# Four zero fills of the cache gradients issued earlier: one behind the softmax, three in the steps of the N passes

## The chip, the cores and the metric

The kernel runs on one core of a Trainium2 chip. TensorE (PE) multiplies matrices, VectorE (DVE) and ScalarE (ACT) work element by element, GpSimd (POOL) and SyncE (SP) are used here almost only to issue DMAs. The DMAs of POOL form one queue (q0 in the profile), those of SP another (q1); both are served by the same 16 DMA engines, which copy between the chip's memory (HBM) and the on-chip buffer (SBUF), or inside HBM. The metric is device time in microseconds, lower is better. Three runs of the kernel before took 599.88, 599.93 and 602.61 us, the median is 599.93 us.

## The reference: what is computed

One token passes through a transformer block with adaptive layer norm, and the gradients of all its inputs are wanted. Cut to what matters:

```python
mod = (silu(c) @ w_mod).reshape(1, 6, 1, -1)      # sa, ca, ga, sb, cb, gb
h = layernorm(x) * (1 + ca) + sa
# attention: 32 query heads, 4 key/value heads, the last W = 4096 of 65536 cached rows
q = (h @ wq).reshape(1, 1, 32, 128)
k = repeat(k_cache[:, :, 65536 - W:, :], 8); v = repeat(v_cache[:, :, 65536 - W:, :], 8)
x = x + ga * ((softmax(q @ k.T * 128 ** -0.5) @ v) @ wo)
h = layernorm(x) * (1 + cb) + sb
x = x + gb * ((sigmoid(h @ w_gate) * (h @ w_up)) @ w_down)      # 1024 -> 3584 -> 1024
# outputs: x and the gradients of x, k_cache, v_cache, wq, wo, w_gate, w_up, w_down, c, w_mod
```

Only the last 4096 rows of the caches take part. So in the gradients of `k_cache` and `v_cache` (out_2 and out_3, 4 x 65536 x 128 in bf16 each) the first 61440 rows of each group are zero, and the kernel must write these zeros: 8 x 15.7 MB, about 126 MB of all the 185.6 MB that it writes to HBM.

## The kernel before

**Stages.** The program is written out by hand in one order for each engine (a manual schedule). Its stages in the profile are: loads, layer norm and the query projection (0 to about 50 us); scores and softmax (50 to 73 us); four N passes of 32 steps each, one pass for each key/value group (73 to 164 us); the B chunks, 64 pieces of 8 matmuls each, with the second layer norm and the modulation between them (164 to 314 us); the feed-forward turns `q` = 0 to 6, one for each 512 of the 3584 columns (320 to about 480 us); the outer products and stores that end the program (480 to 598 us).

**Zero fills.** The zeros are cut into 120 pieces of 1 MB in a list `zleft`. `zero(n, after, big)` (L180 to L208) takes the next `n` pieces and issues a DMA on POOL's queue for each. There are three forms. The plain one (L206) writes 1 MB from `zeros`, an SBUF tile of fp8 zeros that the DMA widens to fp32. With `big=True`, in the N steps and the B chunks, a piece of the `flat` kind is copied from an already zeroed stretch of HBM, with the same widening, so that 0.25 MB is read for 1 MB written (L200). Six pieces, at the positions `NARROW = (15, 45, 75, 93, 103, 113)` of the list, take two DMAs (L191 with 2.5 KB and L194 with 960 KB); the last piece, 119, takes five (L173, L178). A piece keeps its place in the list whatever the place in the program from which it is issued. Pieces 1 to 9 are not of the `flat` kind.

**Where fills are issued.** Tables say how many pieces go where: `Z_Q` in the query projection, `Z_SM` behind the softmax sum, `Z_N[s]` in step `s` = 0 to 127 of the N passes, `Z_B` in the B chunks, `Z_GA`, `Z_CB` and `Z_FOLD` between these and the feed-forward part, `Z_FFN[q]` at four places of turn `q`, `Z_END` behind. `spread(total, n)` deals `total` pieces evenly over `n` steps. Some fills wait for an engine, by an added dependency: the one behind the softmax for DVE's reciprocal `rsum` (L586), those of an N step for a matmul six N matmuls back (`recent(mm, 6)`), those of a B chunk for the chunk's matmul three back. All fills, and nearly all loads and stores, stand in POOL's one queue in program order: a DMA that waits holds up all that are behind it. POOL's DMAs use eight semaphores in turn, so a ninth is issued only when the one eight before it has landed.

**Loads behind the fills.** In POOL's queue, among the N fills and the B fills, stand `load_wo` (L375: `wo` 0, then 4 + g at the end of pass g, and 3), `b_sec` (L378: the sections of `w_mod`, 1 MB each) and the first `load_ug` (L960: `w_up` and `w_gate` of turns 0 and 1). Chunk 9 of the B chunks is the first that needs `wo` 3; `mod_rows(ga)` (L433) needs both `b_sec(2, ...)` loads; `mod_tiles` (L384) needs the first `b_sec(3, ...)` load.

**A feed-forward turn.** In turn `q`, for j = 0 to 7, DVE reduces a tile of `w_up` and `w_gate` (L250) and ACT or DVE overwrites it with its gradient (L281, L246). `store_ug(q, 0, 4)` (L964) follows j = 3, `store_ug(q, 4, 4)` follows j = 7; the fills `z[0]` and `z[1]` stand right behind them. At j = 4 `front(q + 1)` on PE (L1055) needs the `w_up` and `w_gate` of the next turn, which were loaded a turn before. Then come `hh_ops`, `ffn_mm` (L1073), `wd_ttr` and `wd_outer` for turn q + 1, which work on the two halves of `w_down`. There is one buffer for these: SP stores a half (L949), waits until it has landed, and only then loads the same half for the next turn (L946). At the end of turn `q`, `load_ug(q + 2)` waits for `store_ug(q)` to land, because it takes the same buffer:

```python
            if q + 2 < NB:
                load_ug(q + 2, 0, 4)
            wd_outer(q + 1, 1)
            zero(z[2])
            side()
            if q + 2 < NB:
                load_ug(q + 2, 4, 4)
            zero(z[3])
            if q + 2 < NB:
                load_wd(q + 2, 0)
                load_wd(q + 2, 1)
```

Of the kernel before, what the change touches and what calls it, by code (L numbers as in the profile page):

```python
# [41 lines left out]
def spread(total, n):  # L42
    return [(i + 1) * total // n - i * total // n for i in range(n)]
# [6 lines left out]
Z_CB = 1  # L50
Z_Q = [0] * 6 + [1, 3]
Z_KC = [0] * 8
Z_SM = 4
Z_N = spread(31, 128)
Z_B = [n + (i in (31, 38)) for i, n in enumerate(spread(29, 43))] + [1, 1, 1, 1, 0] + [1, 0, 0, 1, 1, 1, 0, 0] + [1, 0, 1, 0, 1, 0, 0, 0]
Z_FOLD = (1, 1, 1, 2)
Z_FFN = [(0, 2, 0, 2), (0, 2, 0, 1), (0, 2, 0, 2)] + [(0, 2, 0, 2)] * 2 + [(1, 1, 1, 3), (1, 2, 1, 0)]
Z_END = (1, 0, 0, 0, 0)
@with_exitstack
def kernel(  # L60
# [121 lines left out]
    def zero(n, after=None, big=False):  # L182
        for _ in range(n):
            if len(zleft) <= keep[0]:
                return
            region, narrow_ = zleft.pop(0)
            first = None
            if narrow_:
                nc.gpsimd.inc_swdge_sem([], [], mode="reset_dge_cursor")
                n = nlen - ncount.pop()  # L190
                first = nc.gpsimd.dma_start(  # L191
                    out=rest[0:NS, 0:nlen * 128].rearrange("p (t x) -> p t x", t=2)[:, :, n * 64:(n + 1) * 64],
                    in_=zeros[0:NS, 0:64].rearrange("p (t x) -> p t x", t=1).broadcast_to([NS, 2, 64]))
                ins = nc.gpsimd.dma_start(  # L194
                    out=region[8:P, :].bitcast(FP32).rearrange("(t p) x -> p t x", t=2),
                    in_=zeros[0:60, :].rearrange("p (t x) -> p t x", t=1).broadcast_to([60, 2, ZW // 2]))
            elif 119 - len(zleft) in UNEVEN:
                first = ins = uneven(region)
            elif big and region.shape[0] == 1:
                ins = nc.gpsimd.dma_start(  # L200
                    out=as_rows(region, BIGP).bitcast(FP32),
                    in_=zero_src[:, 0:P * ZW // 4].rearrange("i (p x) -> (i p) x", p=BIGP).bitcast(FP8))
            else:
                if region.shape[0] == 1:
                    region = as_rows(region, P)
                ins = nc.gpsimd.dma_start(out=region.bitcast(FP32), in_=zeros[:, :])  # L206
            if after is not None:
                dep(first or ins, after)  # L208
# [9 lines left out]
    def new_ps(name="ps"):  # L218
        p, tag = next_pool()
        return p.tile([P, 512], FP32, name=name, tag=tag)  # L220
# [365 lines left out]
    last = nc.vector.reciprocal(out=rsum, in_=ssum)  # L586
    zero(Z_SM, last)
    rs_ps = new_ps("rs_ps")[:, 0:P]
# [125 lines left out]
    def recent(mm, lag):  # L714
        last_mm.append(mm)
        return last_mm[-lag] if len(last_mm) >= lag else last_mm[0]

    for g in range(G):
        nbank = bank_pair("n_ps", g)
        for t_ in range(KT):  # L720
# [7 lines left out]
            for k in range(2):  # L728
                mm = nc.tensor.matmul(nbank[k][:, :], lhsT=k_nat[:, g, t_ * DH:(t_ + 1) * DH],  # L729
                                      rhs=vp[:, t_ % 2, 4 * k:4 * k + 4, :].rearrange("p h d -> p (h d)"),  # L730
                                      start=(t_ == 0), stop=False)
            zero(Z_N[s], recent(mm, 6), True)
            if t_ == 20:
# [387 lines left out]
    for q in range(NB):  # L1121
        z = Z_FFN[q]
        more = q + 1 < NB
# [328 lines left out]
```

## Time and profile before

| What | Value |
|---|---|
| median of three runs | 599.93 us |
| the profiled execution, its own time | 600.48 us |
| its span in the profile | 598.7 us |
| PE, DVE, ACT, POOL busy | 68%, 61%, 43%, 26% of the span |
| moved by DMA | 246.55 MB, mean 412 GB/s |
| POOL's queue, SP's queue (packet time of 16 engines) | 91.4%, 12.8% |
| fills of the plain form (L206) | 45, each 1 MB, median 12.7 us from issue to landing |
| fills of the form in HBM (L200) | 68, median 10.5 us |
| `load_wo` (L375), sections of `w_mod` (L378) | median 8.1 us, 12.0 us |
| stores of `w_down` gradients (L949), loads of `w_down` (L946) | median 10.5 us, 9.6 us |

The packet time of a queue is the time that its packets took, from start to end, as a share of 16 engines' time. Packets of two queues on one engine overlap in it, so the two shares together can pass 100%. "To landing" is counted from the issue to the last of the 16 engines' completion marks, with the time in the queue in it.

### The profile page before, as it was taken

How to read it: one execution, taken by the hardware profiler on the slowest of the kernel's cores; microseconds unless marked ns; L12 is line 12 of the kernel's file. 1: busy time of each engine (PE TensorE's matmuls, PEld its weight loads, DVE VectorE, ACT ScalarE, POOL GpSimd, SP SyncE). 2: the span in 40 equal slices, each digit the busy share in tenths (PEclk: the TensorE clock that was granted, in tenths of full speed). 3: DMA queues.
4: the chain of work that ended last, by engine and by line, in shares of the span. 5: the costliest groups of instructions: out<-in, count | busy, mean ns of one | idle time of the engine just before them, and what ended most of it. 6: DMA issues, size and time to landing. Idle time of an engine off the chain costs nothing. (4 is left out here: it accounts for less than half of the span.)

```text
span 598.7 us, 9909 instructions
## 1 busy us (share of the span) xinstructions
PE 405.1 (68%) x4007; PEld 236.0 (39%) x4036; DVE 362.5 (61%) x677; ACT 259.3 (43%) x398; POOL 153.7 (26%) x258
## 2 busy tenths in 40 slices
PE   3997779998999999997975526254263254984020
PEld 2784433333334545544444525244253234631000
DVE  3765679988730111049266986677866878978160
ACT  3489512554540104311132755464655655893020
POOL 3113113211214113221321333324343154232000
PEclk9997789999999999997996556556555568855555
DMA  8999999999999999999999999999999999999997
GB/s 348 422 420 419 423 458 374 451 440 435 422 413 379 464 427 388 451 422 427 371 412 372 357 411 415 405 409 417 414 415 412 418 418 412 423 424 425 424 416 321
DMA packets 36461, 246.55 MB, mean 412 GB/s; under 512 B 6097, under 2 KB 6097, under 8 KB 21664
## 3 DMA queue, kind: packets, MB, share of 16 engines
q0 software_dynamic: 29120, 218.65, 91.4%
q1 hardware_dynamic: 7248, 27.27, 12.8%
q8 instruction: 31, 0.51, 0.3%
q14 instruction: 14, 0.11, 0.1%
q10 hardware_dynamic: 48, 0.01, 0.0%
HBM read 78.28 MB, written 185.60 MB: 441 GB/s over the span
## 5 line engine op out<-in xcount | busy, mean ns | idle before, releaser
L788 PE MATMUL b_ps<-arena 128*128 128x512 bf16 x493 | 116.1, 383 | 2.6 <-ACT arena L932 1.1
L932 ACT COPY arena<-tp_side 128x1024 bf16<-128x1024 bf16 x62 | 60.9, 1014 | 66.7 <-PE tp_side L931 66.7
L233 DVE TENSOR_TENSOR arena<-arena 128x2048 bf16<-128x2048 bf16 x64 | 77.7, 1224 | 9.0 <-PE n_ps L729 4.0
L250 DVE CUSTOM_DVE_ANT_0 arena<-arena,scr 128x1024 bf16<-128x1024 bf16 x56 | 66.2, 1220 | 9.3 <-ACT scr L1094 9.3
L788 PEld LDWEIGHTS <-arena 128*128 128x128 bf16 x512 | 48.9, 99 | 57.8 <-issue 5.0
L729 PE MATMUL n_ps<-arena 128*128 128x512 bf16 x246 | 66.3, 389 | 4.0 <-DVE arena L233 3.3
L931 PE MATMUL tp_side<-ident_bf,arena 128*128 128x128 bf16 x496 | 55.2, 290 | 13.2 <-DVE arena L233 5.6
L200 POOL DMA_DIRECT2D out_dram<-out_dram x68 | 33.7, 496 | 116.9 <-PE b_ps L788 56.6
L931 PEld LDWEIGHTS <-arena 128*128 128x128 bf16 x496 | 47.1, 135 | 19.2 <-issue 10.3
L1055 PE MATMUL fg<-h_bf,arena 128*128 128x1 bf16 x448 | 15.4, 166 | 48.4 <-DMA arena<-in_B_w_up_dram 29.1
L685 ACT CAST arena<-t_ps 128x512 bf16<-128x512 f32 x56 | 28.9, 598 | 39.9 <-PE t_ps L677 39.9
L281 ACT ACTIVATE arena<-scr,h 128x1024 bf16<-128x1024 bf16 x35 | 38.5, 1143 | 2.7 <-DVE dh2acc L250 2.3
L964 POOL DMA_DIRECT2D out_dram<-arena x28 | 22.1, 795 | 64.7 <-ACT arena L281 45.3
L206 POOL DMA_DIRECT2D out_dram<-zeros x45 | 25.1, 560 | 51.3 <-PE q_ps L433 14.2
L250 DVE CUSTOM_DVE_ANT_0 arena<-arena,b1k 128x1024 bf16<-128x1024 bf16 x24 | 28.4, 1221 | 15.9 <-PE fg L1073 15.9
L1272 ACT ACTIVATE arena<-ps_kv 128x512 bf16<-128x512 f32 x48 | 25.0, 714 | 29.3 <-PE ps_kv L1268 28.5
L1268 PE MATMUL ps_kv<-arena 32*128 32x512 bf16 x64 | 23.9, 546 | 20.1 <-DVE arena L246 19.2
L729 PEld LDWEIGHTS <-arena 128*128 128x128 bf16 x256 | 21.4, 99 | 35.8 <-issue 19.5
L242 DVE CAST arena<-b_ps 128x512 bf16<-128x512 f32 x6 | 4.2, 692 | 50.0 <-PE b_ps L788 50.0
L1055 PEld LDWEIGHTS <-arena 128*128 128x128 bf16 x448 | 13.8, 105 | 51.0 <-DMA arena<-in_B_w_up_dram 30.8
L677 PE MATMUL t_ps<-arena 128*32 128x512 bf16 x256 | 24.1, 399 | 3.4 <-ACT arena L752 2.8
L516 ACT COPY arena<-tp_wq 128x1024 bf16<-128x1024 bf16 x23 | 21.4, 1066 | 7.3 <-PE tp_wq L514 7.3
(314 smaller groups left out, 611.2 us busy)
## 6 DMA issues: line engine op xcount, KB each, us to landing
out_dram<-zeros POOLq DMA_DIRECT2D x45, 1024.0 KB, 12.7
out_dram<-arena POOLq DMA_DIRECT2D x28, 1024.0 KB, 18.6
out_dram<-arena POOLq DMA_DIRECT2D x30, 512.0 KB, 11.2
out_dram<-arena SPq DMA_DIRECT2D x20, 512.0 KB, 10.2
arena<-in_A_wq_dram POOLq DMA_DIRECT2D x8, 1024.0 KB, 21.2
arena<-in_A_wo_dram POOLq DMA_DIRECT2D x8, 1024.0 KB, 8.1
arena<-in_w_mod_dram POOLq DMA_DIRECT2D x7, 1024.0 KB, 12.2
arena<-in_B_w_up_dram POOLq DMA_DIRECT2D x14, 512.0 KB, 11.4
```

The lines of the kernel that those rows point to most:

```text
L200: ins = nc.gpsimd.dma_start(out=as_rows(region, BIGP).bitcast(FP32), in_=zero_src[:, 0:P * ZW // 4].rearrange("i (p x) -> (i p) x", p=BIGP ...
L206: ins = nc.gpsimd.dma_start(out=region.bitcast(FP32), in_=zeros[:, :])
L233: return nc.vector.tensor_tensor(out=out, in0=a, in1=b, op=op)
L250: return nc.vector.tensor_tensor_reduce(out=out, in0=w, in1=b, scale=1.0, scalar=0.0, op0=ALU.mult, op1=ALU.add, accum_out=acc)
L281: return nc.scalar.activation(out=out, in_=b, func=ACT.Copy, scale=col)
L685: nc.scalar.copy(out=o, in_=v)
L729: mm = nc.tensor.matmul(nbank[k][:, :], lhsT=k_nat[:, g, t_ * DH:(t_ + 1) * DH], rhs=vp[:, t_ % 2, 4 * k:4 * k + 4, :].rearrange("p h d -> ...
L788: mm = nc.tensor.matmul(bbank[p][k][:, :], lhsT=a4[:, p, h, :], rhs=wo_t[u][:, a, k * 512:(k + 1) * 512], start=(i == 0 and a == 0), stop= ...
L931: nc.tensor.transpose(tp[:, i * P:(i + 1) * P], blk[:, i * P:(i + 1) * P], ident_bf[:, :])
L932: nc.scalar.copy(out=blk if dst is None else dst, in_=tp[:, :])
L1055: nc.tensor.matmul(gu[:, col:col + 1], lhsT=ug_v[:, q % 2, j // 4, j % 4, k, f0:f0 + 255:2], rhs=h2_bf[:, j:j + 1], start=(j == 0 and i == ...
L1272: nc.scalar.activation(out=o, in_=v, func=ACT.Copy, scale=float(scale))
```

## The change

Four numbers in three tables. `Z_SM` goes from 4 to 5: one more fill behind the softmax. `Z_N` deals 34 fills over the 128 N steps, where it dealt 31. `Z_FFN` loses four: turns 0, 2, 3 and 4 issue one fill as `z[3]`, behind `load_ug(q + 2, 4, 4)`, where they issued two; turn 1 already had one. The counts of all other places stay.

```diff
-Z_SM = 4
-Z_N = spread(31, 128)
+Z_SM = 5
+Z_N = spread(34, 128)
 Z_B = [n + (i in (31, 38)) for i, n in enumerate(spread(29, 43))] + [1, 1, 1, 1, 0] + [1, 0, 0, 1, 1, 1, 0, 0] + [1, 0, 1, 0, 1, 0, 0, 0]
 Z_FOLD = (1, 1, 1, 2)
-Z_FFN = [(0, 2, 0, 2), (0, 2, 0, 1), (0, 2, 0, 2)] + [(0, 2, 0, 2)] * 2 + [(1, 1, 1, 3), (1, 2, 1, 0)]
+Z_FFN = [(0, 2, 0, 1)] * 5 + [(1, 1, 1, 3), (1, 2, 1, 0)]
```

Since the pieces keep their order, every place behind the softmax now issues pieces that stand further on in the list: by one at first, by four from the B chunks to turn 0, by none again from turn 5 on. So the N steps issue pieces 9 to 42 (before 8 to 38), and the narrow piece 93 leaves turn 0 and goes to the end of `Z_FOLD`. By form that makes 41 fills from SBUF (before 45) and 72 in HBM (before 68), with the same six narrow ones and the same last one.

## The prediction

> **What bounds the kernel now.** I read the slices of the page first, then busy time by stage, then the DMA issues of POOL and SP in order of time.
>
> ```profile
> DMA  8999999999999999999999999999999999999997
> ...
> 5.00:66.00 61.00, 49.02 (x677) 37.31 (x677) 34.83 (x71) 41.75 (x60) 13.60 (x25) 0.90 1.04 420
> 66.00:165.00 99.00, 90.10 (x575) 33.45 (x585) 83.03 (x89) 40.04 (x105) 21.15 (x42) 0.98 1.05 428
> 165.00:320.00 155.00, 141.60 (x1071) 72.47 (x1089) 50.55 (x104) 34.86 (x49) 37.85 (x66) 0.98 1.03 416
> 320.00:345.00 25.00, 13.83 (x261) 12.61 (x258) 22.77 (x49) 15.26 (x19) 8.18 (x12) 0.50 1.02 359
> 345.00:500.00 155.00, 69.61 (x1034) 59.07 (x1035) 114.75 (x259) 86.63 (x96) 54.11 (x77) 0.55 1.12 414
> 500.00:590.00 90.00, 40.93 (x397) 21.05 (x396) 55.93 (x106) 39.49 (x74) 17.63 (x29) 0.58 1.03 420
> ```
>
> Columns of the stages: bounds, length, busy time of PE, PEld, DVE, ACT, POOL, granted PE clock, DMA share, GB/s. The DMA engines are busy in every slice, at 414 to 428 GB/s in all stages but one; no compute engine is full for long. So the kernel ends when the DMA engines have moved its 246.55 MB, plus the time in which they had nothing to do. The stage with a hole is 320 to 345, the start of the feed-forward turns:
>
> ```profile
> 320.00:322.00 2.00, 1.62 (x61) 1.53 (x58) 1.95 (x5) 1.23 (x3) 0.00 (x0) 0.50 1.12 418
> 322.00:324.00 2.00, 0.99 (x32) 0.94 (x32) 1.62 (x6) 0.00 (x0) 0.13 (x1) 0.50 0.65 229
> 324.00:326.00 2.00, 0.00 (x0) 0.00 (x0) 1.95 (x4) 0.00 (x0) 0.42 (x1) 0.50 0.83 324
> 326.00:328.00 2.00, 1.76 (x16) 1.73 (x17) 1.03 (x4) 0.65 (x1) 0.66 (x2) 0.50 1.12 422
> 338.00:340.00 2.00, 0.53 (x20) 0.53 (x20) 1.69 (x7) 0.81 (x1) 0.17 (x1) 0.50 0.87 338
> 340.00:342.00 2.00, 2.00 (x34) 2.00 (x32) 2.00 (x3) 0.62 (x1) 2.00 (x4) 0.50 0.48 170
> 342.00:344.00 2.00, 1.21 (x10) 0.78 (x8) 2.00 (x5) 1.81 (x3) 2.00 (x3) 0.50 0.92 309
> ```
>
> The queues ran dry twice: POOL had issued everything and waited for DVE (8.59 us before its issue at 323.87) and ACT (6.53 us before 334.93). At 420 GB/s the five poor windows lost 2 x (191 + 96 + 82 + 250 + 111)/420 = 3.5 us (the 25 us stage as a whole: 25 x 61/420 = 3.6). Elsewhere short windows dip (262 and 206 GB/s in 184 to 188), but their neighbours make it up: 433, 287, 423, 549 GB/s in the four 5 us windows from 180 are 423 on average, since a packet is booked as a whole. I count 0 there, at most 0.7 (85 to 105 averages 405: 20 x 15/420).
>
> **The change, part by part.** (1) Four issues go from turns 0, 2, 3, 4 to 66-165 us. On POOL each costs 0.55 us from SBUF or 0.49 in HBM (L206, L200), and POOL is 21.15 of 99 us busy there: no cost. No bytes are written more or less. A fill in HBM reads 0.25 MB of HBM in place of SBUF; four of the form are added. At what speed? The N stage, mostly that form, moves 428 GB/s, the end, mostly stores from SBUF, 420: -0.05 to +0.2 us for each, taken as 0.
>
> (2) The N stage has no room for them: it issues 4 + 31 fills and 6 `load_wo`, 41 MB of 1.049, which at 428 GB/s is 100.5 us in 99 us. So the added 4.19 MB only lengthen the queue: all that stands behind on POOL's queue lands 4.19/0.42 = 10.0 us later (9.3 if 0.7 us of dips is filled), up to where the queue used to run dry. [...]
>
> (3) Who waits for the late loads? `wo` 3: issued 164.92, landed 8.4 us later at 173.3, then at 183.3; chunk 9 starts at 175.91 + 5 x 1.75 = 184.7 (seven chunks in 12.26 us): no stall. Second half of `ga`: 199.05 + 12.2 + 9.5 = 220.8, its matmuls wanted from 220.1: 0.7 us of PE. First half of `sb`: 252.76 + 10.0 + 9.5 = 272.3, wanted at 270.17: 2.1 us, but PE then stands 2.92 us for DVE at 275.78, which hides it. The last of `load_ug(1)`: 313.97 + 8.4 + 9.5 = 331.9, wanted by 331.6, in a chain that is itself late: 0. The compute chain reaches 322 us some 1 us late (0 to 4), while the queue is 9.3 to 10 us longer: DMA never stands still, so this costs the end nothing. Behind a full POOL queue the ninth DMA waits for its semaphore; what it holds up is in the same queue and would land no sooner.
>
> (4) The hole of 3.5 us is filled, since more than 5 us of queue remain: -3.5.
>
> (5) Turns 1 to 6 start late. With POOL's queue empty the first `store_wd` took 323.60 to 327.52 until its buffer could be loaded again, 3.9 us; under a full queue the next took 343.09 to 353.12, 10.0. The load then landed at 336.7 (9.2 us), and the next store left at 343.09; from a landed load to the store DVE needs 3.2 us (363.29 to 366.50, two L250 and two L246) and PE 0.5 before it, so 2.7 us of the delay are absorbed. The next turn comes about 1 + 6.1 - 2.7 = 4.4 us late. Meanwhile DMA, 3.5 us ahead in the end, needs the turns to follow. A turn's `w_down` loop is store 10.0, load 9.6, then 3.7 = 23.3 us; the five from 343.09 to 467.29 took 124.2. At 23.3 each they take 116.5: 4.4 - 7.7 = -3.3, as good as DMA's lead. With one fill less a turn moves 6.3 + 3.1 MB at 414 GB/s = 22.8 us, so loop and DMA are level. But turns of 23.4, 22.9 and 24.2 us were at the loop already and give nearly nothing back: at worst turn 5 is still 4.4 us late with DMA 3.5 ahead, 7.9 us. The queue that covers it: a `store_ug` landed 11.4 us after issue (median of 340 to 480, L964), 3.4 at the quickest, so 8.0 us of other work stood ahead of it. I take 0.3 us (0 to 3) of new holes.
>
> (6) The last of 16 engines decides. At the end the engines stop between 593.5 and 597 us (share 0.49 in 594 to 596, 0.05 behind); an engine that lags has lost less in the holes. Lost to this: 0.3 us (0 to 2).
>
> Sum on the profiled execution: 600.48 + 0 - 3.5 + 0.3 + 0.3 = 597.6. It lies 0.55 above the median of the runs, so 599.93 - 2.9 = **597.0 us**.
>
> ```profile
> 323.60 3.82 SPq L949 DMA_DIRECT2D out_dram<-arena  x2
> 327.52 3.09 SPq L946 DMA_DIRECT2D arena<-in_B_w_down_dram  x2
> 343.09 3.83 SPq L949 DMA_DIRECT2D out_dram<-arena  x2
> 353.12 2.92 SPq L946 DMA_DIRECT2D arena<-in_B_w_down_dram  x2
> 366.50 4.55 SPq L949 DMA_DIRECT2D out_dram<-arena  x2
> 377.24 4.52 SPq L946 DMA_DIRECT2D arena<-in_B_w_down_dram  x2
> 394.48 3.69 SPq L949 DMA_DIRECT2D out_dram<-arena  x2
> ```
>
> Columns: start, length, SP's queue and line, DMA. Each load of `w_down` follows its store by 10 us or so once the queue is full: that is the loop of step 5.
>
> **Rivals.** *The turns don't catch up (slower).* In the turn 366.50 to 394.48, 28.0 us, the loop was not the bound: the load had landed by 386.8 (377.24 + 9.6), and over all turns PE waited 29.1 us for `w_up` and 19.0 for `w_gate` (L1055). If turns 1 to 5 keep an average t, the change is 4.4 + 5t - 124.2, zero at t = 24.0; above that the engines stand idle for the fills that were moved away. At t = 24.6, between the loop's 23.3 and the 24.8 of before, nearer to the latter since a turn bound by other loads gains little, it is +3.2: 603.1 us. For it: two of five turns took 25.7 and 28.0. Against: that wait is time in the queue, and 1.05 MB less ahead of a load shortens it by 2.5 us. [...]
>
> *The hole only moves (no change).* Bytes are the same; if the thinner queue of turns 2 to 5 runs dry as often as turn 0 did, or the engine that ends last never idled in the hole, the 3.5 us come back: 599.9, within 1.2. For it: loop and DMA are level at 23 us. Against: the 8.0 us of reserve.
>
> *More is gained.* The 0.7 us of dips before 165 us go too, and nothing is lost in (5) and (6): 599.93 - 4.2 = 595.7. It needs every reserve to hold.
>
> **Chances.** Forecast 597.0 (own range 596.0 to 598.7): 0.50. Turns don't catch up, 602.0 to 605: 0.22. Hole moves, 598.7 to 601: 0.20. More gained, 595.3 to 596: 0.08. The bound of 0.5%, about what a measurement of this kernel can tell from no change, is 3.0 us: 596.93 and 602.93. Faster: 0.28 of the forecast, whose middle lies on the bound, and 0.08 = 0.36. Same: 0.22 of the forecast, all 0.20 of the second = 0.42. Slower: 0.22. The range runs from 595.5 to 603.4: it leaves out the upper part of the slower case and the last of the gain, some 0.15.
>
> **What would show it.** Right: no window of 2 us under 400 GB/s between 322 and 346; loads of `wo` and `w_mod` (L375, L378) land 6 to 10 us later after issue than 8.1 and 12.0; the first `store_wd` waits 10 us, not 3.9; the five turns from the second `store_wd` take 115 to 118 us; the mean rate rises to 414 GB/s. Wrong: windows well under 400 GB/s between 400 and 470 (the hole moved, or the turns don't catch up: then the five turns take over 120 us), or PE idle at L788 or L433 for many us before 320.

## The result and the profile after

| | before | after |
|---|---|---|
| median, runs beside each other | 600.06 us (599.88 to 602.61, 4 runs) | 593.69 us (593.46 to 594.23, 4 runs) |
| the profiled execution, its span | 600.48, 598.7 us | 593.46, 591.7 us |

The ratio is 0.9885, 95% interval 0.9858 to 0.9913: the change is faster, by 6.4 us in the medians and 7.0 us between the two profiled executions. The forecast was 597.0 us, range 595.5 to 603.4. Its direction was right; the gain was more than twice the 2.9 us forecast, and the time lies below the range.

The page of the profile after, its span, the DMA row of its slices, its DMA totals and two of its rows of DMA issues (count, KB of each, median us from issue to landing):

```profile
span 591.7 us, 9934 instructions
...
DMA  8999999999999999999999999999999999999998
...
DMA packets 36013, 246.55 MB, mean 417 GB/s; under 512 B 6097, under 2 KB 6097, under 8 KB 21664
...
arena<-in_A_wo_dram POOLq DMA_DIRECT2D x8, 1024.0 KB, 13.5
arena<-in_w_mod_dram POOLq DMA_DIRECT2D x7, 1024.0 KB, 19.0
```

The bytes are the same and the mean rate rose from 412 to 417 GB/s, more than the forecast's 414. In the median the loads behind the fills take 5.4 us (`wo`) and some 7 us (`w_mod`) longer from issue to landing than before; the forecast had named 6 to 10 us for both. The stages of the profile after (bounds, length, busy time of PE, PEld, DVE, ACT, POOL, granted PE clock, DMA share, GB/s):

```profile
5.00:66.00 61.00, 48.86 (x677) 37.23 (x677) 34.80 (x71) 41.66 (x59) 13.59 (x25) 0.90 1.04 420
66.00:165.00 99.00, 91.13 (x586) 33.39 (x585) 82.98 (x89) 40.08 (x105) 22.95 (x46) 0.98 1.05 431
165.00:320.00 155.00, 140.83 (x1074) 70.92 (x1072) 49.02 (x102) 34.90 (x48) 37.89 (x66) 0.99 1.03 423
320.00:345.00 25.00, 11.26 (x217) 10.28 (x215) 18.90 (x41) 12.34 (x16) 6.50 (x10) 0.50 1.14 403
345.00:500.00 155.00, 75.28 (x1138) 64.58 (x1138) 121.34 (x272) 93.09 (x105) 55.09 (x78) 0.56 1.10 412
```

The stage with the hole went from 359 to 403 GB/s. But the two stages ahead of it also went up, from 428 to 431 and from 416 to 423, and at 420 GB/s that is (99 x 3 + 155 x 7)/420 = 3.3 us (2.5 by the exact times below) for which the forecast had counted nothing. The five windows of 2 us that made the hole, in the profile after:

```profile
322.00:324.00 2.00, 1.56 (x59) 1.47 (x56) 1.53 (x6) 1.16 (x3) 0.00 (x0) 0.50 1.06 397
324.00:326.00 2.00, 0.99 (x32) 0.94 (x32) 1.62 (x6) 0.00 (x0) 0.19 (x1) 0.50 1.10 410
...
338.00:340.00 2.00, 1.01 (x8) 0.74 (x7) 1.96 (x4) 1.81 (x3) 0.41 (x1) 0.50 1.24 416
340.00:342.00 2.00, 0.00 (x0) 0.00 (x0) 1.48 (x6) 0.74 (x1) 0.24 (x1) 0.50 1.05 397
342.00:344.00 2.00, 0.00 (x0) 0.00 (x0) 0.00 (x0) 0.00 (x0) 2.00 (x4) 0.50 1.02 375
```

Before they moved 229, 324, 338, 170 and 309 GB/s. Three of the five are still a little under the 400 GB/s that the forecast had named as its sign, but the DMA share is above 1.00 in each. PE does nothing from 340 to 344 us, later than before, and the DMA engines work on all the same. The loop of `w_down` after (start, length, SP's queue and line):

```profile
325.54 3.81 SPq L949 DMA_DIRECT2D out_dram<-arena  x2
335.95 5.46 SPq L946 DMA_DIRECT2D arena<-in_B_w_down_dram  x2
348.72 4.31 SPq L949 DMA_DIRECT2D out_dram<-arena  x2
...
465.19 3.69 SPq L949 DMA_DIRECT2D out_dram<-arena  x2
```

The first store now waits 335.95 - 325.54 = 10.4 us, the next turn starts 5.6 us later than before (348.72 against 343.09), and the five turns take 116.5 us against 124.2, so that the last store leaves 2.1 us earlier.

**Where the time came from.** Two figures were worked out from the packet records of each trace. The *lead* of a kernel is the time at which the packets of the profile before had moved so many MB, less the time at which this kernel's had. *Lost time* is the time in which a DMA engine had no packet, as a mean over the 16 engines; where two packets overlap on one engine (the DMA share is 1.03 to 1.14 in the stages above) it hides the other's rest, so it is a lower bound.

| MB moved (time in the profile before) | 30 (74) | 40 (98) | 90 (216) | 130 (311) | 145 (351) | 190 (461) | 245 (592) | span |
|---|---|---|---|---|---|---|---|---|
| lead of after, us | 0.0 | 0.55 | 1.71 | 2.51 | 5.91 | 5.93 | 5.66 | 7.0 |

So 2.5 us were gained ahead of 311 us and 3.4 in the hole; 0.25 were lost again, all behind 461 us; and 1.4 were gained behind 592 us, where the engines run out. The lost time shows less than that:

| lost time, us | 85 to 100 us | 100 to 311 us | the hole, 311 to 351 us | behind 570 us |
|---|---|---|---|---|
| before | 0.20 | 0.50 | 2.64 | 2.3 |
| after | 0.00 | 0.00 | 0.02 | 1.0 |

### The profile page after: what moved, and what is told of

It reads as the page before. It is cut to its first block, busy times and chain, and to the rows that moved or that the text cites. A ratio compares the mean times of both kernels' runs of the same rounds, so it can differ in the third digit from the quotient of the medians.

```text
span 591.7 us, 9934 instructions
## 1 busy us (share of the span) xinstructions
PE 406.7 (69%) x4036; PEld 236.4 (40%) x4036; DVE 361.8 (61%) x677; ACT 259.9 (44%) x398; POOL 153.3 (26%) x258
## 4 chain that ended last, share of the span: by engine, by line
DMA 37%; PE 32%; DVE 14%; ACT 8%; issue 4%; POOL 0%; ACTq 0%; DVEq 0%; POOLq 0%; SPq 0%
DMA out_dram<-out_dram 10%; DMA out_dram<-arena 9%; PE n_ps L729 9%; DMA arena<-in_B_w_gate_dram 7%; DMA arena<-in_w_mod_dram 6%; PE b_ps L788 4%; DVE arena L250 4%; DVE arena L246 4%; PE t_ps L677 4%; DMA out_dram<-zeros 3%; ACT arena L516 2%; DVE arena L233 2%; PE tp_side L931 2%; PE bc_ps L337 1%; DMA arena<-in_B_w_down_dram 1%
## 5 line engine op out<-in xcount | busy, mean ns | idle before, releaser
L729 PE MATMUL n_ps<-arena 128*128 128x512 bf16 x256 | 67.7, 388 | 3.6 <-DVE arena L233 3.3
L200 POOL DMA_DIRECT2D out_dram<-out_dram x72 | 35.5, 494 | 128.2 <-PE n_ps L729 54.3
L206 POOL DMA_DIRECT2D out_dram<-zeros x41 | 23.0, 565 | 43.1 <-PE q_ps L433 14.3
```

The lines of the kernel that those rows point to most:

```text
L200: ins = nc.gpsimd.dma_start(out=as_rows(region, BIGP).bitcast(FP32), in_=zero_src[:, 0:P * ZW // 4].rearrange("i (p x) -> (i p) x", p=BIGP ...
```

## The experiments

Each kernel was timed beside the kernel before on the same chip, in a few series; a difference with a sign is worked out from the ratio. The median of before is 600.06 us beside the change and 601.69 to 602.11 us in the later series, so kernels of two series are best compared by their traces. Lines of the diffs are against the changed kernel; `...` marks what is left out, and what isn't shown is as there. Three theories were tested. *Queue*: the end follows from the time that the engines lose wherever POOL's queue is short, and any place ahead of these serves for the fills. *Hole*: only the stretch of 320 to 345 us counts. *Lighter turns*: the turns gain because they hold less.

**Two fills in place of four**, into the N steps, from turns 3 and 4.

```diff
-Z_SM = 5
-Z_N = spread(34, 128)
-Z_FFN = [(0, 2, 0, 1)] * 5 + [(1, 1, 1, 3), (1, 2, 1, 0)]
+Z_SM = 4
+Z_N = spread(33, 128)
+Z_FFN = [(0, 2, 0, 2), (0, 2, 0, 1), (0, 2, 0, 2)] + [(0, 2, 0, 1)] * 2 + [(1, 1, 1, 3), (1, 2, 1, 0)]
```

> Two fills move, from turns 3 and 4 into the N passes (33 instead of 31). Theory Q (queue): what counts is DMA time lost anywhere before 350 us while POOL's queue is short, 5.9 us in all in the kernel before, and each moved fill buys back 2.5 us of it until it is used up. Then two fills give -5.0 us (-4 to -5.5). Theory H (hole only): only the hole at 320 to 345 us counts, 3.5 us, and the rest of the -6.4 us comes from something else in the change; two fills fill the hole, so -3.5 us (-3 to -4). Theory T (lighter turns): the gain comes from each of turns 0, 2, 3, 4 having one fill less, 1.6 us each; two turns give -3.2 us.

596.55 us, ratio 0.9924 (0.9906 to 0.9942), -4.6. A little more than the hole alone should give, as the queue theory had it. Its lead is only 3.8 us at 351 us, and 0.66 us are still lost in the hole.

**Four fills put close ahead of the hole**, into the last B chunks; softmax and N steps as before the change.

```diff
-Z_SM = 5
-Z_N = spread(34, 128)
+Z_SM = 4
+Z_N = spread(31, 128)
-Z_B = ... + [1, 0, 0, 1, 1, 1, 0, 0] + ...
+Z_B = ... + [1, 1, 1, 1, 1, 1, 1, 1] + ...
```

> The same four fills leave the same turns, but go to B chunks 49, 50, 54 and 55 (about 280 to 300 us) instead of the softmax and the N passes. Theory Q: the hole at 320 to 345 is filled and what is lost from 285 on, but the 1.7 us that the engines had lost by 285 us stay lost: -4.3 us (-3.5 to -5). Theory H: -3.5 us plus the unknown rest, which would stay if it belongs to the turns (-6.4) and go if it belongs to the N passes (-3.5). Theory T: -6.4 us, since the turns are the same.

596.58 us, ratio 0.9914 (0.9897 to 0.9932), -5.2, a little more than the -3.5 to -5 expected. This is the part of the gain that can be had behind 280 us: the lead is -0.2 us until 263 us, 4.2 at 351, 4.6 at 592. The profile is of its fastest run (594.62 us; the other five took 596.5 to 596.7). Between the two profiles the change is 1.1 us ahead, which must come from ahead of 280 us; by the medians, of two series, it is 2.9.

**The four fills taken from turns 5 and 6**; turns 0 to 4 as heavy as before.

```diff
-Z_FFN = [(0, 2, 0, 1)] * 5 + [(1, 1, 1, 3), (1, 2, 1, 0)]
+Z_FFN = [(0, 2, 0, 2), (0, 2, 0, 1), (0, 2, 0, 2)] + [(0, 2, 0, 2)] * 2 + [(1, 1, 1, 1), (0, 1, 1, 0)]
```

> The same four fills are added behind the softmax and in the N passes, but they are taken from turns 5 and 6 (two each), and turns 0 to 4 keep theirs. Theory Q: the queue before 350 us is as long as in the changed kernel, so -6.4 us (-5.5 to -7). Theory H: about the same, -3.5 or better. Theory T: turns 0 to 4 are as heavy as before, so nothing is gained, within 1 us of before.

597.55 us, ratio 0.9935 (0.9917 to 0.9953), -3.9: the queue theory's -6.4 was missed. But its lead is 6.75 us at 461 us, more than the change's 5.9, with turns that hold as much as before, so the gain does not come from lighter turns. It is lost again where the fills are missing. Its windows there:

```profile
480.00:484.00 4.00, 0.00 (x0) 0.00 (x0) 4.00 (x7) 4.00 (x5) 0.00 (x0) 0.50 0.97 345
484.00:488.00 4.00, 0.00 (x0) 0.00 (x0) 3.89 (x10) 4.00 (x5) 1.60 (x2) 0.50 0.91 322
488.00:492.00 4.00, 2.07 (x18) 1.53 (x22) 2.41 (x12) 1.45 (x2) 3.47 (x6) 0.50 0.76 269
```

DVE and ACT work without a rest, POOL issues nothing from 472.3 to 484.1 us while it waits for ACT, and the lead falls from 6.6 to 3.4 us between 485 and 496: the hole has moved to the end of the turns.

**The four fills put behind the turns**: lighter turns alone.

```diff
-Z_SM = 5
-Z_N = spread(34, 128)
-Z_END = (1, 0, 0, 0, 0)
+Z_SM = 4
+Z_N = spread(31, 128)
+Z_END = (1, 2, 2, 0, 0)
```

> The same four fills leave turns 0, 2, 3, 4, but go behind the feed-forward part (two more at each of the second and third places of Z_END), not ahead of it. Theory Q: the queue before 350 us is as short as before and the 5.9 us stay lost: 0 us (-0.5 to +2, more if the turns' queue runs dry too). Theory H: 0 as well. Theory T: -6.4 us.

601.24 us, ratio 0.9992 (0.9978 to 1.0006), -0.5: no change, 2.9 us are still lost in the hole. Lighter turns give nothing by themselves.

**The softmax fill alone**, taken from turn 4.

```diff
-Z_N = spread(34, 128)
-Z_FFN = [(0, 2, 0, 1)] * 5 + [(1, 1, 1, 3), (1, 2, 1, 0)]
+Z_N = spread(31, 128)
+Z_FFN = [(0, 2, 0, 2), (0, 2, 0, 1), (0, 2, 0, 2), (0, 2, 0, 2), (0, 2, 0, 1), (1, 1, 1, 3), (1, 2, 1, 0)]
```

> One fill alone: the fifth behind the softmax, taken from turn 4; N steps and turns 0 to 3 as before. Queue theory (the end follows from the engine time lost where POOL's queue is short, and 1 MB of queue is 2.5 us of cover from its place on): the 1 MB stays in the queue from 75 us to turn 4, so it covers the starts of 93 and 186 us and 2.5 of the 3.5 us hole: about -3.0 us (-2 to -4), and the before's own scatter of 600 to 602.7 us goes, because the queue no longer runs dry at 86 to 97 us when the softmax sum is late. Theory that only the hole of 320 to 345 us matters: -2.5. Theory that each fill behind the softmax does its work at 85 to 97 us alone: -0.5 to -1.

598.23 us, ratio 0.9949 (0.9928 to 0.9969), -3.1. The size is as expected, but split in another way: the lead is already 2.2 us at 311 us and grows by only 0.6 in the hole, where 1.76 us are still lost. The fill moved forward put the engines ahead once, by about its own 1.05 MB (2.5 us at 420 GB/s), and what it had covered ahead of 311 us was no longer in the queue behind. The scatter that should have gone did not go: its runs lie at 597.49 to 600.07.

**The change without its softmax fill**, four fills in the N steps.

```diff
-Z_SM = 5
-Z_N = spread(34, 128)
+Z_SM = 4
+Z_N = spread(35, 128)
```

> The change without its softmax part: four fills in the N steps (35 in place of 31), four behind the softmax as before, turns as in the change. Queue theory: the hole and the stalls from 100 us on are covered as in the change (-3.5 and some -1.5), the stall at 86 to 97 us stays: -5 us against before (-4 to -6), with the wide scatter of before kept (some 2 us between runs). Theory that only the hole matters: equal to the change, -6.4, with its narrow scatter. Theory that the softmax fill gave most of the unexpected 3.5 us: -3.

596.50 us, ratio 0.9909 (0.9888 to 0.9931), -5.5, and in absolute time 2.8 us above the change. Between 85 and 100 us its profile loses 1.94 us, the change's none; from there on it gains as the change does. So the one fill behind the softmax is worth some 2 us in these profiles and 2.8 in the medians. How much it is worth differs from run to run: three other kernels with four softmax fills lose only 0.20 to 0.53 us there (the table below).

**Another choice of turns**: one fill each from turns 3, 4 and 5, one from the end of turn 6.

```diff
-Z_FFN = [(0, 2, 0, 1)] * 5 + [(1, 1, 1, 3), (1, 2, 1, 0)]
+Z_FFN = [(0, 2, 0, 2), (0, 2, 0, 1), (0, 2, 0, 2), (0, 2, 0, 1), (0, 2, 0, 1), (1, 1, 1, 2), (1, 1, 1, 0)]
```

> Four fills behind the softmax and in the N steps as in the change, but taken from other turns: one each from turns 3, 4, 5 and one from the end of turn 6, so that turns 0 to 2 stay as heavy as before. Queue theory: the lead of 6.7 us that the run with all four taken from turns 5 and 6 had at 470 us is kept if no turn's own queue runs dry: -6.5 to -7.5; if the fill missing in turn 6 opens a hole at 480 to 495 us again, half of that run's 3.3 us: -5. Theory that lighter turns 0 to 4 carry the gain: -2 to -3.

594.65 us, ratio 0.9886 (0.9867 to 0.9905), -6.8 by the ratio, but 1.0 us above the change's own time of another series, and 1.1 above the next kernel, which ran beside it. The lead is 6.55 us at 461 us and 5.3 at 496: a smaller loss where the other kernel with fills taken from turns 5 and 6 had its hole.

**The narrow pieces kept at their places in the program**, to see whether the gain at the end comes from them.

```diff
-NARROW = (15, 45, 75, 93, 103, 113)
+NARROW = (17, 49, 79, 96, 105, 113)
```

> The change, with the six narrow pieces kept at the places of the program where before issued them (positions 17, 49, 79, 96, 105, 113 of the list instead of 15, 45, 75, 93, 103, 113). If the 1.0 to 1.3 us that the change gained behind 570 us come from the narrow pieces being issued earlier (another engine ahead at the end): +1.0 us against the change, -5.4 against before. If they come from the engines losing less to dry queues: equal to the change within 0.5 us, -6.4 against before.

593.54 us, ratio 0.9871 (0.9849 to 0.9894): equal to the change in absolute time, with the same lead (5.75 us at 245 MB, 7.1 at the end). The narrow pieces have no part in it.

**Six fills**, two more from turns 2 and 4.

```diff
-Z_N = spread(34, 128)
-Z_FFN = [(0, 2, 0, 1)] * 5 + [(1, 1, 1, 3), (1, 2, 1, 0)]
+Z_N = spread(36, 128)
+Z_FFN = [(0, 2, 0, 1), (0, 2, 0, 1), (0, 2, 0, 0), (0, 2, 0, 1), (0, 2, 0, 0), (1, 1, 1, 3), (1, 2, 1, 0)]
```

> Six fills moved in place of four: one behind the softmax, five in the N steps (36), two more taken from turns 2 and 4, which then issue none behind their second load of w_up and w_gate. Queue theory: in the change's profile the engines stand empty for only 0.1 us between 5 and 570 us, so there is nothing left to cover: equal to the change within 1 us (-6.4 against before, -5.5 to -7.5), or worse by 1 to 3 us if turns 2 to 5 now run dry. Theory that every fill moved forward is worth its share (six move 6/4 of four): -9.6.

596.21 us, ratio 0.9911 (0.9893 to 0.993), -5.4, 2.5 us above the change and 2.7 above the next kernel, which ran beside it: past the best dose. The lead is 6.8 us at 388 us, then 5.5 at 436, 4.9 at 473 and 4.4 at 496. What POOL waited for from 340 to 500 us, in the change and then here (total us, times, longest):

```profile
POOL out_dram L964 <- ACT arena L281: 48.8, 6, 10.1
```

```profile
POOL out_dram L964 <- ACT arena L281: 60.9, 7, 12.8
```

Before it was 38.7. The queue's head waits longer for ACT's gradients. This fits the slower rival of the forecast, "the turns don't catch up": the turns' own work sets a pace of 23 us (352.93 to 468.06 us for the five here), turns 2 and 4 now hold 9.4 - 1.05 = 8.4 MB, 20 us at 414 GB/s, and the lead melts. With four fills it does not yet decide. The lost time from 351 to 500 us is only 0.45 us, though: that these waits cost the 2.4 us of lead is argued, not shown.

**Two fills behind the softmax and two in the N steps.**

```diff
-Z_SM = 5
-Z_N = spread(34, 128)
+Z_SM = 6
+Z_N = spread(33, 128)
```

> The change with two of its four fills behind the softmax instead of one, and two in the N steps (33). Queue theory: the one fill there already covers the late start of the N steps (of the profiles with five, none lost more than 0.3 us at 85 to 100 us; those with four lost 0.2 to 1.9), so equal to the change within 0.5 us: -6.4. Theory that the place behind the softmax is worth 2.8 us for each fill, the distance between the change and the same four fills without it: -9.

593.51 us, ratio 0.9868 (0.9846 to 0.9891): equal to the change in absolute time. One fill there is enough.

**All fills of the N steps from SBUF.**

```diff
-            zero(Z_N[s], recent(mm, 6), True)
+            zero(Z_N[s], recent(mm, 6))
```

> The change with the fills of the N steps all written from the zero tile in SBUF, none copied in HBM; the B chunks as they were. Form theory (part of the 3.5 us more than predicted comes from the four fills that changed to the form in HBM, and that form is quicker): slower than the change by at least 4 us, since some 25 fills change back. Queue theory: the form is worth -0.05 to +0.2 us for each fill as predicted: within 1.5 us of the change (the sign open), at most 25 x 0.2 = 5 us faster.

594.25 us, ratio 0.988 (0.9861 to 0.9899), 0.7 us above the kernel with two softmax fills, beside which it ran. 32 fills changed their form (L200 went from 72 to 40), where some 25 were expected, so one is worth about 0.02 us: the form has no part in the result.

**The kernel before once more**, for a second profile: its runs lie in two groups, at 599.9 to 600.9 and 601.7 to 602.9 us.

> The kernel before once more, for a second profile of it: its runs lie either at 599.9 to 600.9 or at 601.7 to 602.9 us. Clock theory (the matmuls that sum the values, L625, end 2 us later when TensorE is granted half its clock between 68 and 73 us, the first fill of the N steps is then issued 2 us later, and the four fills behind the softmax don't last so long): a profile at 602 us shows PEclk 0.5 in 68 to 72 us, the first N fill issued at 75 in place of 72.9 us, and 1.5 to 2.5 us of lost engine time at 85 to 98 us; one at 600 us shows the full clock there and 0.2 us lost, as the first profile of before. The theory falls if a profile at 602 us shows the full clock at 68 to 72 us, or one at 600 us the half clock.

602.52 us. Windows of the first profile of before, at 600.48 us:

```profile
68.00:70.00 2.00, 1.54 (x32) 0.78 (x36) 2.00 (x6) 1.56 (x8) 0.91 (x2) 1.00 1.01 414
70.00:72.00 2.00, 2.00 (x40) 0.85 (x32) 1.80 (x2) 1.73 (x9) 0.00 (x0) 1.00 1.17 442
...
86.00:88.00 2.00, 1.89 (x8) 0.67 (x7) 2.00 (x2) 0.00 (x0) 0.49 (x1) 1.00 0.86 360
...
94.00:96.00 2.00, 1.09 (x5) 0.43 (x5) 2.00 (x3) 0.00 (x0) 0.05 (x1) 1.00 0.74 217
```

and of the second, at 602.52 us:

```profile
68.00:70.00 2.00, 1.16 (x10) 0.38 (x13) 1.55 (x5) 0.80 (x4) 1.56 (x3) 0.50 1.04 426
70.00:72.00 2.00, 2.00 (x24) 0.79 (x20) 2.00 (x4) 2.00 (x11) 0.00 (x0) 0.51 1.11 422
...
86.00:88.00 2.00, 2.00 (x6) 0.73 (x5) 1.43 (x2) 0.00 (x0) 0.50 (x1) 0.50 0.02 0
...
94.00:96.00 2.00, 1.83 (x16) 0.56 (x15) 1.97 (x4) 0.00 (x0) 0.30 (x1) 1.00 0.00 0
```

The granted PE clock between 68 and 72 us is 1.00 in the one and 0.50 in the other; with half the clock PE gets through 24 matmuls in 70 to 72 us instead of 40. From 86 to 88 and from 94 to 96 us the engines of the second stand still. POOL's issues behind the softmax, first and second profile (start, length, line, what the idle time before it waited for):

```profile
66.78 2.12 POOL L206 DMA_DIRECT2D out_dram<-zeros  x4 [7.42 <-DVE rsum L586]
72.94 0.53 POOL L206 DMA_DIRECT2D out_dram<-zeros  x1 [4.03 <-PE n_ps L729]
```

```profile
67.43 2.12 POOL L206 DMA_DIRECT2D out_dram<-zeros  x4 [7.42 <-DVE rsum L586]
75.02 0.53 POOL L206 DMA_DIRECT2D out_dram<-zeros  x1 [5.46 <-PE n_ps L729]
```

The first fill of the N steps waits for PE, comes 2.1 us later, and the four softmax fills don't last until the steps have caught up. Its lead is -2.5 us at 40 MB and stays there (-2.2 at the end): the distance of the two groups. The second profile came out as the clock theory had it (the first was known when the theory was made): the time at which the full clock sets in goes with the group, and the waits behind it give the distance. With one profile for each group this is well supported, not proved. Over all kernels, the fifth fill covers the stall:

| granted clock is full again from | lost at 85 to 100 us with four softmax fills | with five |
|---|---|---|
| 67 to 68 us | 0.20, 0.53, 0.36 (before; two fills; last B chunks) | 0.00 in each of five profiles |
| 72 to 74 us | 1.71, 1.94, 2.52 (fills behind the turns; N only; before again) | 0.32, 0.24 (narrow pieces; all from SBUF) |

The kernel with two more fills behind the softmax, six in all there, had its full clock from 74 us and loses 0.00 there. The scatter of the runs does not always go with the stall: three kernels with five softmax fills (the ones with fills taken from turns 5 and 6, with the softmax fill alone, and with another choice of turns) still spread by 1.9 to 2.6 us, and why is not shown.

Lead in us over the first profile of before, of all kernels:

| | 40 MB (98) | 90 (216) | 130 (311) | 145 (351) | 190 (461) | 205 (496) | 245 (592) | span |
|---|---|---|---|---|---|---|---|---|
| the change | 0.55 | 1.71 | 2.51 | 5.91 | 5.93 | 5.83 | 5.66 | 7.0 |
| two fills | -0.48 | 0.65 | 1.18 | 3.83 | 3.74 | 3.71 | 3.76 | 3.8 |
| last B chunks | -0.18 | -0.20 | 0.62 | 4.17 | 4.58 | 4.57 | 4.58 | 5.9 |
| taken from turns 5, 6 | 0.57 | 1.72 | 2.53 | 6.16 | 6.75 | 3.37 | 2.81 | 3.3 |
| behind the turns | -1.86 | -1.96 | -1.91 | -2.12 | -2.19 | -2.01 | -1.60 | -1.0 |
| softmax alone | 0.62 | 1.64 | 2.22 | 2.82 | 2.85 | 2.74 | 2.82 | 3.0 |
| N only | -1.61 | -0.39 | 0.33 | 3.84 | 3.86 | 3.44 | 3.40 | 4.6 |
| other turns | 0.58 | 1.78 | 2.61 | 5.83 | 6.55 | 5.27 | 5.11 | 5.7 |
| narrow pieces | 0.13 | 1.22 | 1.92 | 5.54 | 5.92 | 5.84 | 5.75 | 7.1 |
| six fills | 0.80 | 2.01 | 3.19 | 6.61 | 5.23 | 4.41 | 4.44 | 4.6 |
| two behind the softmax | 0.78 | 1.90 | 2.73 | 5.83 | 6.02 | 5.95 | 5.78 | 6.9 |
| all from SBUF | 0.09 | 0.69 | 1.37 | 4.99 | 5.16 | 5.03 | 4.95 | 5.8 |
| before again | -2.52 | -2.68 | -2.70 | -2.21 | -2.19 | -2.19 | -2.17 | -2.0 |

No version beat the change; the ones with narrow pieces at their old places and with two softmax fills are level with it.

## Why the prediction was off

**Step 4, the hole: right.** -3.5 forecast, 3.4 us of lead between 311 and 351 us.

**The dips ahead of 311 us: this is the term that failed.** The forecast put it as "I count 0 there, at most 0.7". The profile after shows 2.5 us. It judged short windows by their neighbours and by 420 GB/s, and so could only find the time in which engines stand idle. That time is 0.70 us ahead of 311 us in the profile before, as much as the forecast's upper end, but by luck: 0.20 of it lie at 85 to 100 us, where the forecast saw all of its 0.7, and 0.47 at 184 to 188, where it saw none. The other 1.8 us were gained where the count finds no engine without a packet: some 0.8 us of them between 216 and 311 us, where neither profile loses any time. Only long windows of the same work show it, before and then after:

```profile
66.00:165.00 99.00, 90.10 (x575) 33.45 (x585) 83.03 (x89) 40.04 (x105) 21.15 (x42) 0.98 1.05 428
165.00:311.00 146.00, 135.90 (x996) 68.86 (x1014) 48.09 (x98) 32.14 (x44) 35.26 (x62) 0.98 1.03 417
```

```profile
66.00:165.00 99.00, 91.13 (x586) 33.39 (x585) 82.98 (x89) 40.08 (x105) 22.95 (x46) 0.98 1.05 431
165.00:311.00 146.00, 136.43 (x1027) 68.28 (x1025) 47.84 (x98) 32.22 (x44) 35.71 (x63) 1.00 1.03 422
```

That is 0.7 + 1.7 = 2.4 us. The one fill behind the softmax gives most of it: alone it has a lead of 2.2 us at 311 us. That a fuller queue brings it is borne out by the kernel with its fills in the last B chunks, which also gains 0.8 us between 216 and 311 us, and by the one with its fills behind the turns, which gains nothing there. Why less was moved there while no engine is counted idle stays open. One of the stalls that do count could have been found in POOL's issues before: a fill at 181.56, then no transfer until a narrow fill at 185.02 (2.5 KB) and 185.63 (960 KB), with 0.7 MB (1.6 us) left in POOL's queue at 185, by the bytes issued less the bytes moved.

```profile
181.56 0.49 POOL L200 DMA_DIRECT2D out_dram<-out_dram  x1 [1.24 <-PE b_ps L788]
185.02 0.61 POOL L191 DMA_DIRECT2D out_dram<-zeros  x1 [2.97 <-PE b_ps L788]
185.63 0.68 POOL L194 DMA_DIRECT2D out_dram<-zeros  x1
186.30 1.67 POOL L206 DMA_DIRECT2D out_dram<-zeros  x3
```

At 186 to 187 us the engines moved 68 GB/s; the lost time from 184 to 188 us is 0.47 us, and 0 in the change, whose queue held 4.4 MB at 185. The forecast had set this dip to 0 because 180 to 200 averages 423 GB/s; the same window averages 420 after, so a window of 20 us doesn't tell.

**Step 6, the last engine: wrong sign.** +0.3 (0 to 2) was forecast, -1.4 measured. The windows before and after in which the engines run out:

```profile
592.00:594.00 2.00, 0.00 (x0) 0.00 (x0) 0.00 (x0) 0.00 (x0) 0.00 (x0) 0.50 0.99 412
594.00:596.00 2.00, 0.00 (x0) 0.00 (x0) 0.00 (x0) 0.00 (x0) 0.00 (x0) 0.50 0.49 205
596.00:599.00 3.00, 0.00 (x0) 0.00 (x0) 0.00 (x0) 0.00 (x0) 0.00 (x0) 0.50 0.05 19
```

```profile
587.00:589.00 2.00, 0.00 (x0) 0.00 (x0) 0.00 (x0) 0.00 (x0) 0.00 (x0) 0.50 0.98 414
589.00:592.00 3.00, 0.00 (x0) 0.00 (x0) 0.00 (x0) 0.00 (x0) 0.00 (x0) 0.50 0.15 63
```

After, the engines end closer together: the last store's completions (L1277) spread over 4.0 us before and over 2.1 after. The forecast held that an engine that lags had lost less in the holes and would gain less by filling them; the end that came closer together speaks against it, though the records don't say which engine lags. Of the kernels whose queue did not run dry behind 311 us, most lose 0.9 to 1.0 us at the end (the change, last B chunks, N only, narrow pieces), those with a dry spell there 1.6 to 2.3. The kernels with two more softmax fills and with all N fills from SBUF have no such spell and lose 1.2 and 1.4, so this is a tendency and not a rule. Why the engines drift apart stays open.

**Step 5, the turns: right.** The first store waited 10.4 us (10.0 forecast), the next turn came 5.6 us late (4.4), the five took 116.5 (115 to 118, from 23.3 each), and no lead was lost up to 461 us and 0.1 us up to 496 (0.3 forecast). From 2.5 MB in POOL's queue on, the store's wait did not grow with the bytes there: it was 9.8 to 10.7 us in the profile before with 3.1 to 3.7 MB issued and not yet moved (means over the waits), 9.7 to 10.5 after with 2.5 to 2.8, and 3.9 with 0.8.

**Steps 1 to 3: right in the main.** The form of a fill is worth 0.02 us. The N stage moved 431 GB/s, so 3 x 99 us = 0.3 MB of the 4.19 found room there and the rest lengthened the queue. The last load of `wo` ahead of the B chunks took 17.9 us to land, 9.5 more than before (10.0 forecast); in the median the delays were smaller. The late loads cost PE 2.1 us at L433 and 0.7 at L384 (about 1, 0 to 4 forecast), the first `store_wd` left 1.9 us later, and the end lost nothing by it.

In sum: -2.5 - 3.4 + 0.25 - 1.4 = -7.05, against 600.48 - 593.46 = 7.02. With the forecast's -3.5 and +0.3 for steps 4 and 5 alone it would have been -3.2: the two failed terms, the dips and the end, make the difference.

**The rivals.** "More is gained" named the right direction and half of the place, but took the dips for 0.7 us and had nothing of the end. "The hole only moves" appeared when the fills came from turns 5 and 6. "The turns don't catch up" appeared with six fills. The first was a real mechanism, one place away from the change; the second fits what was measured, one dose away.

**Base.** The forecast's time was tied to a median of 599.93. In 35 further runs beside the experiments, in three series, before lay at 601.7 to 602.1 in the median, since its runs fall into two groups; the four runs of the change lie within 0.8 us. Against these medians the gain is about 8 us.

## What to carry to other kernels

Where the DMA engines set the end, price a queue by all its short places, not by the one that shows: compare the stage's rate with the best rate of the same mix, and look at the gaps between issues against the MB left in the queue. A transfer moved forward put the engines ahead once here, by about its own bytes (the softmax fill alone, 1.05 MB: a lead of 2.8 us); it covered stalls in the order in which they came until it was used up (2.2 us ahead of 311 us, 0.6 in the hole), and taken from a place that was itself short of transfers it opened a stall there, as the fills from turns 5 and 6 did (the lead fell from 6.6 to 3.4 us). A kernel whose runs fall into two groups may be telling where its cover is thin, as before did at 85 to 100 us (0.20 us lost in one profile, 2.52 in the other).

## What was not expected of the hardware

**The full clock of TensorE can set in at another time in another execution of the same program.** It was full again from 67.4 us in one profile of before and from 72.0 in the other. In the first, as in the profile after, all its steps are 3.4 us or a multiple apart (6.8, 13.7 and 37.5 us among those of the first); in the second, the two returns to the full clock that its windows show, at 72.0 and 89.0 us, are 17.0 us apart. A DMA that waits for a matmul passed the delay on: the first fill of the N steps left at 75.02 us, not at 72.94, and the spans are 600.7 and 598.7 us.

**More was gained than the time in which engines stand idle.** Between before and the change the lost time differs by 5.6 - 1.0 = 4.6 us, the end by 7.0. The rate can also differ with hardly an engine idle: from 390 to 440 us the change and then the kernel with six fills moved

```profile
390.00:440.00 50.00, 22.68 (x344) 20.23 (x342) 38.84 (x80) 28.43 (x32) 19.33 (x27) 0.50 1.07 413
```

```profile
390.00:440.00 50.00, 25.59 (x426) 23.20 (x424) 38.68 (x82) 29.88 (x35) 17.52 (x25) 0.53 1.06 403
```

That is some 1.2 us, with less than 0.2 us lost by the count in all of 351 to 470. What the other 2.4 us between before and the change are (packets that overlap and so hide a rest, or a lower rate with fewer in flight) can't be told from these records.
